# A decode step bound by its K and V loads: q from the even and odd columns of wq beside w3, the first K in two halves, rows 16 apart with one output transfer, and wo in six pieces

## The chip, the cores and the metric

The kernel runs on one core of a Trainium2 chip. The core has five engines that run their own instruction streams and meet through semaphores: TensorE (PE), VectorE (DVE), ScalarE (ACT), GpSimd (POOL) and SyncE (SP), which here issues nearly all transfers. Sixteen DMA engines move the data between the chip's main memory (HBM) and the on-chip memory (SBUF, 128 partitions); matmuls write into PSUM (eight banks of 512 fp32 values per partition). The metric is the device time of one execution in microseconds; the time of a kernel is the median of its runs. One further execution was profiled, and all durations come from that one.

## The reference

One token of each of two sequences passes a grouped-query attention over a cache of 32,768 positions, an MLP branch gates it, and the input is added.

```python
x = A_x                                   # (2, 1, 512), bf16
xn = layernorm(x)
q = xn @ wq                               # 32 heads of 128
# 8 K/V heads, each shared by 4 query heads
p = softmax(q . k_cache * 128**-0.5)      # k_cache, v_cache: (2, 8, 32768, 128), bf16
s = (p . v_cache) @ wo                    # wo: (4096, 512)
z = layernorm(xn)
h2 = gelu(z @ w3) @ w4                    # w3: (512, 1792), w4: (1792, 512)
g = silu(xn + h2)
out = x + s * g
```

In the reference's second branch there is also a term through w1 and w2 (h shifted along the sequence, then w2, added to xn before the second layernorm). With a sequence of one position all four shifts fill in zeros, so that term is zero, and the kernel leaves w1 and w2 out. The K and V caches are 268 MB of the 280.5 MB that are read.

## The kernel before

**Units.** The work is 16 units n, one for each pair of batch (n % 2) and K/V head (n // 2). Each has 8.39 MB of K and 8.39 MB of V. Both are loaded as 128 partitions of contiguous rows. `vbuf` holds one V. `kbuf` holds three halves of a K (each `CW` columns): K of an even unit lies in halves 0 and 1, of an odd unit in halves 1 and 2, and `halves(b)` gives the order in which a unit's halves are used, so that the half which the next K overwrites is used first.

**One unit.** `scores(n)`: VectorE transposes K in eight tiles of 128 x 2048 words (line 471) into two buffers `ktb`; TensorE multiplies each with the query heads in `qz` (line 483). `softmax(n)`: VectorE takes the maximum (line 496), small matmuls bring it together and spread it, ScalarE takes the exponential (line 506), VectorE transposes the weights into `pT` (line 512). `values(n)`: TensorE multiplies them with V (line 524). `unit_sum` and `unit_out` collect the unit's four heads into `oQ`; they are run inside the next unit.

**Order.** A recording layer, `Plan`, takes each operation with the regions that it reads and writes (`P.op`, line 40), works out the semaphore waits, and keeps one list for each engine in the order of recording. SyncE, ScalarE and GpSimd get their lists flat (`emit_flat`, line 97). TensorE and VectorE get loops over the units (`emit_looped`): `fit` (line 101) finds for each wait a line in the loop's counter, and waits that hold only for the first round are put ahead of the loop. TensorE's program up to the wo rows stands in a loop of two visits whose body runs in the second alone (lines 163 to 165); behind it follow the instructions from the one labelled "stop" on, the first of the wo rows.

**Transfers.** SyncE's queue holds in order: wq (into half 2 of `kbuf`), w3 (into the first columns of `vbuf`), K of unit 0 (all of it, line 337), the second half of V of unit 0, its first half (after w3 has been used), then K and V of each next unit, each waiting until its place has been used: K(n+1) for VectorE's transposes of the first-used half of K(n), V(n+1) for TensorE's `values(n)`. K of the last unit comes in two halves with the semaphores "ka" and "kb". At the end follow w4 (into half 0) and wo (into half 1), the latter in the five pieces of `wo_cuts` (line 240): 22, 4, 2, 2 and 2 rows of 512 columns on each partition.

**Head.** ScalarE issues the loads of x: `x_bf` (two rows) and `x4` (each sequence cut in four pieces of 128, put on partitions 32 j + b). Two layernorms run on VectorE with ScalarE's square root; xn and the second layernorm's result go through `xx` into `z4`, by two transfers on ScalarE's queue, in the same placing. From `z4` come `zT` (columns for the matmuls) and `xrep`. `q_job` (line 424): TensorE multiplies with wq into eight banks of 512 columns (line 432), ScalarE copies each bank to bf16 with the innermost pairs pulled apart (line 442) into `q_row`, which lies in `ktb[0]`, VectorE transposes four pieces (line 447) into `q_turn`, in `ktb[1]`, and copies out `qp` (line 449); then it clears six PSUM regions (line 453). `mlp_in` (line 555) multiplies with w3.

**Tail.** After `values(15)`: w4's product (line 608), `gather` (line 616: it adds the four partition groups by a matmul with `sel`), the last unit's sum, a transpose, and the permutation that makes `oP`, the attention result as columns by wo row (lines 649 to 656). `wo_rows` (line 626) multiplies the first rows into four partition groups of `wP`, VectorE copies these to `wsum` (line 662), and a `gather` adds the groups into `s_ps`. `wo_last` (line 637) multiplies the last rows into `s_ps` directly, in four 128-column pieces a row; the order on TensorE is rows of pieces 1 and 2, `wo_last` of pieces 3 and 4, `gather`, `wo_last` of piece 5. VectorE multiplies with the gate (line 668) and adds x (line 669), and SyncE and ScalarE each issue the output of one sequence and wait for it.

Of the kernel before, what the change touches and what calls it, by code (L numbers as in the profile page):

```python
# [26 lines left out]
class Plan:  # L27
# [3 lines left out]
    def __init__(self, nc, sems):  # L31
# [6 lines left out]
        self.turn, self.inner = {}, None  # L38
# [58 lines left out]
    def emit_flat(self, eng):  # L97
        for o in self.ops[eng]:
            self.emit_one(o, sorted(o.waits.items()))

    def fit(self, points, first):
# [17 lines left out]
        for k, w in points.items():  # L119
            for s, v in w.items():  # L120
                if k[0] == first and s not in line:
                    ahead[s] = max(ahead.get(s, 0), v)
# [46 lines left out]
    def emit_rounds(self, eng, kind, ops, first, last, ahead, rounds, segments, plans, stop):  # L169
# [6 lines left out]
        with self.nc.Fori(0, len(rounds), 1, engines=[kind], hint_back_edge=True) as i:  # L176
            for seg, fits in zip(segments, plans):
                if len(seg[0]) == 1:
                    o, line = rounds[0][seg[0][0]], fits[0]
                    self.emit_one(o, [(s, i * step + base) for s, (base, step, _) in line.items()])  # L180
# [12 lines left out]
def kernel(  # L193
# [40 lines left out]
    assert NCH == 2 and NB == NS and NU % 2 == 0 and FK <= 16 and W3 <= CW and FK * D <= CW  # L234
# [30 lines left out]
    sel = sb("sel", [128, 4, rep], F32)  # L265
    mask = sb("mask", [128, 4], F32)
    x_bf = sb("x_bf", [B, D], BF16)
    xf = sb("xf", [B, D], F32)
    xn = sb("xn", [B, D], F32)
    xx = sb("xx", [B, 4, 2, D // 4], F32)  # L270
# [3 lines left out]
    oP = sb("oP", [128, B, NR], BF16)  # L274
# [27 lines left out]
                 "wo0", "wo1", "wo2", "wo3", "wo4", "out0", "out1"]  # L302
# [14 lines left out]
    def load(sem, out_ap, in_ap, wr, rd=(), eng="SP"):  # L317
        e = {"SP": nc.sync, "ACT": nc.scalar}[eng]
        P.op(eng, lambda: e.dma_start(out=out_ap, in_=in_ap), [al(r) for r in rd],
# [14 lines left out]
    def load_k(n):  # L334
        c0 = place(n % 2, 0)
# [33 lines left out]
    for b in range(B):  # L369
        load("x4", x4[b:128:32, :], A_x[b, 0, :].rearrange("(j c) -> j c", j=4), [f"x4_{b}"],  # L370
             rd=["x4"], eng="ACT")

    dve(lambda: V.tensor_copy(out=xf[:, :], in_=x_bf[:, :]), ["x_bf"], ["xf"])
# [16 lines left out]
    layernorm(quarters(xn[:, :]), "xn", xf[:, :], "xf", 1)  # L390
    act(lambda: A.copy(out=xx[:, :, 0, :], in_=quarters(xn[:, :])), ["xn"], ["xx0"])
    dve(lambda: V.tensor_copy(out=identf[:, :], in_=ident[:, :]), ["ident"], ["identf"])
    layernorm(xx[:, :, 1, :], "xx1", xn[:, :], "xn", 2)
    for b in range(B):
        load("z4", z4[b:128:32, :, :].rearrange("j s c -> j (s c)"),
             xx[b:b + 1, :, :, :].rearrange("o j s c -> o j (s c)"), [f"z4_{b}"], rd=["xx0", "xx1", "z4"], eng="ACT")
# [8 lines left out]
    sel2 = sel[:, :, :].rearrange("p i h -> p (i h)")  # L405
    dve(lambda: V.tensor_add(out=sel2, in0=identf[:, 0:16], in1=identf[:, 32:48]), ["identf"], ["sel"])
# [308 lines left out]
```

## Time and profile before

| | |
|---|---|
| Median of 3 runs | 659.19 us (658.31 to 659.75) |
| The profiled execution | 658.29 us |
| Its span, first to last instruction | 656.3 us |
| Read from HBM | 280.50 MB, 427 GB/s over the span |
| DMA queue of SyncE (q1), share of 16 engines | 99.0% |
| TensorE matmuls busy | 401.8 us (61%) |
| VectorE busy | 385.6 us (59%) |
| ScalarE busy | 47.2 us (7%) |
| GpSimd busy | 6.7 us (1%) |
| Mean granted TensorE clock | 0.818 of full speed |

A row of the timeline gives the start and the length in microseconds, the engine, the line, the operation, the tiles (out <- in) with their shape, the count of instructions merged, and in brackets how long the engine had been idle before and what released it. PEld is the loading of weights into TensorE. "SPq" and "ACTq" are the instruction queues of SyncE and ScalarE, which issue transfers; a merged row "x2" of these runs from the first issue's start to the last one's end. A releaser is inferred: where an instruction waits for several semaphores, the last one by the profile is named.

### The profile page before, as it was taken

To read this page: it belongs to the slowest core of one execution; us is meant where nothing else is said; L and a number is where in the kernel's file an instruction comes from. 1 tells how busy PE (TensorE), PEld (TensorE's weight loads), DVE (VectorE), ACT (ScalarE), POOL (GpSimd) and SP (SyncE) were. 2 spreads that over 40 slices of the span, in tenths; PEclk is the share of its full clock that TensorE was granted. 3 is DMA by queue.
4 is the path that set the end of the run, shared out by engine and by line. 5 is a ranking of instruction groups with operands and counts; after the bars stand their busy time and mean duration, and the time that the engine had idled before them with its cause. 6 is when DMAs were issued, how large, how long until landed. Compare 5 with 4: busy or idle time off the path is not lost.

```text
span 656.3 us, 5842 instructions
## 1 busy us (share of the span) xinstructions
PE 401.8 (61%) x2291; PEld 153.4 (23%) x2291; DVE 385.6 (59%) x305; ACT 47.2 (7%) x67; POOL 6.7 (1%) x27
## 2 busy tenths in 40 slices
PE   0547583775648466573855657385565847656855
PEld 0213231231213122121322213122121312212322
DVE  4277481945739184572927648193663819367962
ACT  1910000000000000000000000000000000000011
POOL 1000000000000000000000000000000000000000
PEclk9879698776979878697886869788696978869887
DMA  8999999999999999999989999999999999999996
GB/s 365 452 417 473 387 447 431 399 447 447 447 415 415 447 447 447 403 427 447 447 387 443 448 447 439 391 447 447 447 439 391 447 447 447 431 399 445 449 402 285
DMA packets 6102, 280.54 MB, mean 427 GB/s; under 512 B 714, under 2 KB 724, under 8 KB 1236
## 3 DMA queue, kind: packets, MB, share of 16 engines
q1 hardware_dynamic: 6056, 280.50, 99.0%
q8 instruction: 1, 0.02, 0.0%
q10 hardware_dynamic: 44, 0.01, 0.0%
q14 instruction: 1, 0.01, 0.0%
HBM read 280.50 MB, written 0.00 MB: 427 GB/s over the span
## 4 chain that ended last, share of the span: by engine, by line
DMA 63%; DVE 14%; PE 14%; issue 4%; ACT 4%; ACTq 0%; POOL 0%; DVEq 0%; POOLq 0%; SPq 0%
DMA kbuf<-in_A_k_cache_dram 59%; DVE ktb L471 12%; PE banks L483 11%; DMA vbuf<-in_A_v_cache_dram 4%; ACT ktb L442 3%; PE banks L524 2%; DMA z<-xx 1%; PE banks L626 0%; PE banks L432 0%; DVE banks L453 0%; DVE acs L534 0%; ACT L658 0%; ACT L384 0%; DVE ktb L447 0%; DVE pT L512 0%
## 5 line engine op out<-in xcount | busy, mean ns | idle before, releaser
L471 DVE STREAM_TRANSPOSE ktb<-kbuf 128x2048 uint32<-128x2048 uint32 x128 | 287.3, 2288 | 164.1 <-DMA kbuf<-in_A_k_cache_dram 159.0
L483 PE MATMUL banks<-ktb,qz 128*128 128x512 bf16 x1024 | 273.1, 416 | 151.0 <-DVE ktb L471 150.3
L483 PEld LDWEIGHTS banks<-ktb,qz 128*128 128x128 bf16 x1024 | 97.2, 103 | 328.3 <-issue 186.1
L524 PE MATMUL banks<-vbuf,pT 128*16 128x512 bf16 x1024 | 89.6, 527 | 15.3 <-DVE rS L513 12.7
L524 PEld LDWEIGHTS banks<-vbuf,pT 128*16 128x16 bf16 x1024 | 31.2, 116 | 67.0 <-issue 55.9
L548 ACT CAST oQ<-banks 128x4 bf16<-128x4 f32 x16 | 2.6, 162 | 511.1 <-PE banks L545 511.1
L496 DVE TENSOR_REDUCE m<-banks 128x1 f32<-128x1024 f32 x16 | 19.6, 1225 | 32.1 <-PE banks L483 32.1
L512 DVE STREAM_TRANSPOSE pT<-pr 128x1024 bf16<-128x1024 bf16 x16 | 19.9, 1245 | 20.4 <-ACT pr L506 20.4
L509 PE MATMUL banks<-S,headf 128*128 128x1 f32 x32 | 8.0, 319 | 23.8 <-ACT pr L506 23.8
L506 ACT ACTIVATE pr<-banks,nb 128x1024 bf16<-128x1024 f32 x16 | 17.8, 1114 | 38.7 <-DVE nb L505 38.7
L432 PE MATMUL banks<-kbuf,xrep 128*128 x32 | 10.0, 486 | 15.7 <-DVE xrep L420 15.7
L442 ACT CAST ktb<-banks 128x512 bf16<-128x512 f32 x8 | 18.4, 2752 | 10.9 <-PE banks L432 10.9
L538 DVE TENSOR_REDUCE acr<-acs 128x128 f32<-128x512 f32 x17 | 17.6, 1038 | 0.6
L497 PE MATMUL banks<-identf,m 128*1 128x128 f32 x16 | 4.3, 270 | 19.2 <-DVE m L496 19.2
L534 DVE SCALAR_TENSOR_TENSOR acs<-banks,rS,mask 128x512 f32<-128x512 f32 x17 | 12.1, 714 | 4.9 <-PE banks L524 4.9
L447 DVE STREAM_TRANSPOSE ktb<-ktb 128x1024 bf16<-128x1024 bf16 x4 | 5.0, 1245 | 17.0 <-ACT ktb L442 17.0
L509 PEld LDWEIGHTS banks<-S,headf 128*128 128x128 f32 x32 | 6.6, 259 | 25.2 <-ACT pr L506 25.2
L502 PE MATMUL banks<-ones_f,gx 1*128 1x1 f32 x32 | 6.0, 256 | 9.9 <-DVE gx L500 9.9
L457 POOL TENSOR_TENSOR qz<-qp,qm 128x64 bf16<-128x64 bf16 x17 | 5.0, 293 | 623.4 <-PE banks L483 588.3
L555 PE MATMUL banks<-vbuf,zT 128*2 128x448 bf16 x16 | 3.4, 983 | 12.7 <-DVE banks L453 12.7
L432 PEld LDWEIGHTS banks<-kbuf,xrep 128*128 128x128 bf16 x32 | 3.8, 118 | 21.4 <-issue 19.3
L498 DVE TENSOR_REDUCE gm<-banks 1x4 f32<-1x128 f32 x16 | 4.5, 278 | 5.8 <-PE banks L497 5.8
(75 smaller groups left out, 60.4 us busy)
## 6 DMA issues: line engine op xcount, KB each, us to landing
vbuf<-in_A_v_cache_dram SPq DMA_DIRECT2D x2, 4096.0 KB, 30.3
kbuf<-in_A_k_cache_dram SPq DMA_DIRECT2D x2, 4096.0 KB, 22.1
kbuf<-in_A_wq_dram SPq DMA_DIRECT2D x1, 4096.0 KB, 13.4
kbuf<-in_A_wo_dram SPq DMA_DIRECT2D x1, 2816.0 KB, 31.0
vbuf<-in_B_w_dram SPq DMA_DIRECT2D x1, 1792.0 KB, 17.2
kbuf<-in_B_w_dram SPq DMA_DIRECT2D x1, 1792.0 KB, 28.1
kbuf<-in_A_wo_dram SPq DMA_DIRECT2D x3, 256.0 KB, 30.5
kbuf<-in_A_wo_dram SPq DMA_DIRECT2D x1, 512.0 KB, 30.0
```

The source lines that it names most:

```text
L432: r = T.matmul(banks[:, bass.ds(c * 512, 512)], lhsT=xrep[:, k, :, :].rearrange("p i w -> p (i w)"), rhs=kb[:, bass.ds(c * 512 + (2 * CW + ...
L442: act(lambda c=c: A.copy(out=q_row[:, 512 * c:512 * (c + 1)].rearrange("p (x two w) -> p x w two", two=2, w=32), in_=banks[:, 512 * c:512 ...
L471: dve(lambda i=i, c0=c0: V.transpose(out=ktb[i][:, :], in_=kbuf[:, c0:c0 + KG * GT * Dh].bitcast(U32)), [kreg(c0, KG * GT * Dh)], [f"ktb{i ...
L483: r = T.matmul(sc[:, bass.ds(half, HW)].rearrange("p (t k) -> p t k", k=32), lhsT=qz[:, k, off:off + 128], rhs=kv[:, k // 2, k % 2, :, :], ...
L496: dve(lambda: V.tensor_reduce(out=m1[:, :], in_=sc[:, :], axis=AX.X, op=ALU.max), ["sc"], ["m1"], "max")
L502: pe(lambda: T.matmul(bc, lhsT=gx[:, :, :].rearrange("o x h -> o (x h)"), rhs=ones_f[0:1, 0:1], start=True, stop=True), ["gx", "ones_f"], ...
L506: act(lambda: A.activation(out=pr[:, :], in_=sc[:, :], func=ACT.Exp, bias=nb[:, 0:1], scale=inv_sqrt_dh, accum_out=S1[:, :]), ["sc", "nb"] ...
L509: pe(lambda: T.matmul(sS, lhsT=headf[:, :, :].rearrange("p x h -> p (x h)"), rhs=S1[:, :], start=True, stop=True), ["headf", "S1"], [rO], "S")
L512: dve(lambda: V.transpose(out=pT[:, :, :].rearrange("p t r -> p (t r)"), in_=pr[:, :]), ["pr"], ["pT"], "pT")
L524: r = T.matmul(acc[32 * j:32 * j + 16, :].rearrange("p (i d) -> p i d", d=Dh), lhsT=pT[:, half * GT + u, r0:r0 + 16], rhs=vv[:, x, u, :, : ...
L534: dve(lambda: V.scalar_tensor_tensor(out=acs[:, :, :], in0=acc[:, :].rearrange("p (i d) -> p i d", d=Dh), scalar=rS[:, 0:1], in1=mask[:, : ...
L538: dve(lambda: V.tensor_reduce(out=acr[:, :], in_=acs[:, :, :].rearrange("p i d -> p d i"), axis=AX.X, op=ALU.add), ["acs"], ["acr"], "acr")
```

## The change

Seven edits, made together:

- **q by parities.** TensorE's product with wq takes every second column of wq as the moving operand (`[:, 0:1023:2]`), four blocks of even columns into four banks, then four of odd ones into the other four, by two nested loops. ScalarE's copies then read and write runs of 32 neighbouring values.
- **q beside w3.** `q_row` and `q_turn` lie in `vbuf` behind w3's columns instead of in `ktb`. The first half of V of unit 0, which overwrites both, waits for TensorE's product with w3 and for VectorE's copy of `qp`. `xf`, `xn` and `xx` become parts of `ktb[1]`.
- **The first K in halves.** K of unit 0 is loaded by two transfers of 4.19 MB, the half used first under "k", the other under "kb". VectorE's loop waits for "kb" at its fixed value in each round (`fixed` in `fit`).
- **Rows 16 apart.** The two sequences lie on partitions 32 j and 32 j + 16 instead of 32 j and 32 j + 1. Small products write M = 17 rows instead of 2, `oP` has 32 columns for each row of wo (cleared once on GpSimd), `sel` has 32 columns, and three of the six clears of PSUM go. `x4` is loaded by one transfer.
- **One output transfer.** SyncE issues both sequences' output as one transfer of eight rows; GpSimd waits for it, and the block is left without GpSimd's drain.
- **wo in six pieces** of 16, 8, 2, 2, 2 and 2 rows. `wo_rows` takes the first 24 rows, `wo_last` the last 8; the `gather` stands after `wo_last` of pieces 3 and 4 and ahead of pieces 5 and 6.
- **Order of writing out.** The first loads and clears of SyncE, ScalarE and GpSimd are written out ahead of TensorE's and VectorE's programs, the rest of their lists after them; each of the three engines gets a branch in between. The loop of two visits on TensorE stays.

```diff
-    wo_cuts = [0, NR - 10, NR - 6, NR - 4, NR - 2, NR]
+    wo_cuts = [0, NR - 16, NR - 8, NR - 6, NR - 4, NR - 2, NR]
...
+                if k[0] == first and s in self.fixed:
+                    line[s] = (v, 0, 0)
+                elif k[0] == first and s not in line:
                     ahead[s] = max(ahead.get(s, 0), v)
...
-        if n < NU - 1:
+        if 0 < n < NU - 1:
...
-        for sem, c in zip(("ka", "kb"), halves(n % 2)):
+        for sem, c in zip(("ka" if n else "k", "kb"), halves(n % 2)):
...
+    pool(lambda: G.memset(oP[:, :, :], 0.0), wr=["oP"])
+    load("x4", x4[0:128:16, :], A_x[:, 0, :].rearrange("b (j c) -> j b c", j=4), ["x4_0"], rd=["x4"], eng="ACT")
...
-        q_row, q_turn = (ktb[i][:, :].bitcast(BF16) for i in range(2))
+        q_row, q_turn = (vbuf[:, W3 + HD * i:W3 + HD * (i + 1)] for i in range(2))
...
-            with nc.Fori(0, 8, 1, engines=[mybir.EngineType.PE]) as c:
+            with nc.Fori(0, 2, 1, engines=pes) as e, nc.Fori(0, 4, 1, engines=pes) as h:
...
-                        rhs=kb[:, bass.ds(c * 512 + (2 * CW + k * HD), 512)],
+                        rhs=kb[:, bass.ds(h * 1024 + (e + (2 * CW + k * HD)), 1023)][:, 0:1023:2],
...
-                out=q_row[:, 512 * c:512 * (c + 1)].rearrange("p (x two w) -> p x w two", two=2, w=32),
-                in_=banks[:, 512 * c:512 * (c + 1)].rearrange("p (x w two) -> p x w two", two=2, w=32)),
+                out=q_row.rearrange("p (h x two w) -> p h two x w", h=4, two=2, w=32)[:, c % 4, c // 4, :, :],
+                in_=banks[:, 512 * c:512 * (c + 1)].rearrange("p (x w) -> p x w", w=32)),
...
-        for t, name in ((hP, "hP"), (acc, "acc"), (mD, "mD"), (wP, "wP"), (s_ps, "s_ps"), (gP, "mA")):
+        for t, name in ((acc, "acc"), (mD, "mD"), (wP, "wP")):
...
-                wP[32 * j:32 * j + B, :], lhsT=oP[:, :, r], rhs=kbuf[:, CW + r * D:CW + (r + 1) * D],
+                wP[32 * j:32 * j + M, :], lhsT=oP[:, r, 0:M], rhs=kbuf[:, CW + r * D:CW + (r + 1) * D],
...
-    for b, eng in enumerate(("SP", "ACT")):
-        load(f"out{b}", out[b, 0, :].rearrange("(j c) -> j c", j=4), out_bf[b:128:32, :], [f"out{b}"],
-             rd=["out_bf"], eng=eng)
+    load("out0", out[:, 0, :].rearrange("b (j c) -> j b c", j=4), out_bf[0:128:16, :], ["out0"], rd=["out_bf"])
...
-    with tc.tile_critical():
-        P.emit_flat("SP")
-        P.emit_flat("ACT")
-        P.emit_flat("POOL")
-        nc.sync.wait_ge(P.sems["out0"], 16)
-        nc.scalar.wait_ge(P.sems["out1"], 16)
+    with tc.tile_critical(no_gpsimd_drain=True):
+        for e, n in early.items():
+            P.emit_flat(e, 0, n)
         P.step = dict(steps, k=16, v=16)
         P.emit_looped("PE", mybir.EngineType.PE)
         P.step = {s: 2 * v for s, v in dict(steps, k=16, v=16).items()}
         P.emit_looped("DVE", mybir.EngineType.DVE)
+        for e, n in early.items():
+            P.emit_flat(e, n, None)
+        nc.gpsimd.wait_ge(P.sems["out0"], 16)
```

More of the change, by code (lines that the diff above doesn't have):

```diff
@@ L264 @@
     headm = sb("headm", [128, rep], F32)
-    sel = sb("sel", [128, 4, rep], F32)
+    sel = sb("sel", [128, 32], F32)
     mask = sb("mask", [128, 4], F32)
     x_bf = sb("x_bf", [B, D], BF16)
-    xf = sb("xf", [B, D], F32)
-    xn = sb("xn", [B, D], F32)
-    xx = sb("xx", [B, 4, 2, D // 4], F32)
+    rows = ktb[1][0:B, :].bitcast(F32)
+    xf, xn = rows[:, 0:D], rows[:, D:2 * D]
+    xx = rows[:, 2 * D:4 * D].rearrange("b (j s c) -> b j s c", j=4, s=2)
+    r_xf, r_xn, r_x0, r_x1 = (("ktb1", 2 * D * i, 2 * D * (i + 1)) for i in range(4))
     oQ = sb("oQ", [128, B, NR], BF16)
@@ L368 @@
     pool(lambda: G.memset(qz[:, :, :], 0.0), wr=["qz"])
[L369 to L373, printed above, removed]
+    pool(lambda: G.memset(oP[:, :, :], 0.0), wr=["oP"])
+    load("x4", x4[0:128:16, :], A_x[:, 0, :].rearrange("b (j c) -> j b c", j=4), ["x4_0"], rd=["x4"], eng="ACT")
+    early = {e: len(P.ops[e]) for e in ("SP", "ACT", "POOL")}
+    dve(lambda: V.tensor_copy(out=xf[:, :], in_=x_bf[:, :]), ["x_bf"], [r_xf])
     def quarters(a):
```

71 lines of the change are left out of this document (39 added, 32 removed).

## The prediction

> **What bounds the kernel now.** I read the page first (engine shares, the 40 slices, the chain that ended last), then the stages, then the DMA issues with their landings, and last the timeline of the head and of the tail.
>
> ```profile
> span 656.3 us, 5842 instructions
> DMA  8999999999999999999989999999999999999996
> q1 hardware_dynamic: 6056, 280.50, 99.0%
> DMA 63%; DVE 14%; PE 14%; issue 4%; ACT 4%; ACTq 0%; POOL 0%; DVEq 0%; POOLq 0%; SPq 0%
> L471 DVE STREAM_TRANSPOSE ktb<-kbuf 128x2048 uint32<-128x2048 uint32 x128 | 287.3, 2288 | 164.1 <-DMA kbuf<-in_A_k_cache_dram 159.0
> ```
>
> The queue of SyncE, q1, fills 99% of the span, and VectorE, which must transpose every K tile, spends 159.0 us waiting for K to land. So the first question on any edit is whether it changes the stream of bytes, and the second whether it changes what comes after the last byte. The stages (columns: stretch, length, busy time of five engines, TensorE clock, DMA share, GB/s):
>
> ```profile
> 36.00:76.00 40.00, 27.34 (x151) 9.56 (x151) 26.50 (x24) 2.66 (x5) 0.59 (x2) 0.80 1.03 439
> 76.00:116.00 40.00, 23.25 (x135) 8.91 (x135) 23.34 (x17) 1.37 (x3) 0.29 (x1) 0.84 0.98 423
> 116.00:316.00 200.00, 125.53 (x687) 47.94 (x688) 120.22 (x85) 6.84 (x15) 1.47 (x5) 0.80 1.01 435
> 636.00:650.00 14.00, 9.25 (x113) 3.44 (x115) 5.47 (x13) 2.92 (x5) 0.00 (x0) 0.74 0.94 397
> 651.00:652.00 1.00, 0.76 (x22) 0.25 (x20) 0.69 (x1) 0.00 (x0) 0.00 (x0) 0.50 0.16 59
> ```
>
> The long middle runs at 435 GB/s, and the head, 36 to 76 us, already at 439. The only weak place before the tail is 76 to 116 us with 423: at 435 its bytes would need 1.1 us less (40 x 12/435). The last bytes come just after 651 us (59 GB/s in the last row). What is left is a fixed tail of some 5 us.
>
> The SyncE issues of the head, and the landings of the four transfers after the first three (the last column of a landing row is us from issue to landing):
>
> ```profile
> 2.33 39.79 SPq L319 DMA_DIRECT2D vbuf<-in_A_v_cache_dram  x2
> 50.72 0.33 SPq L319 DMA_DIRECT2D kbuf<-in_A_k_cache_dram  x1
> 74.20 0.33 SPq L319 DMA_DIRECT2D vbuf<-in_A_v_cache_dram  x1
> ```
> ```profile
> vbuf<-in_A_v_cache_dram SPq DMA_DIRECT2D x1, 4096.0 KB, 45.2
> vbuf<-in_A_v_cache_dram SPq DMA_DIRECT2D x1, 4096.0 KB, 15.4
> kbuf<-in_A_k_cache_dram SPq DMA_DIRECT2D x1, 25.9
> vbuf<-in_A_v_cache_dram SPq DMA_DIRECT2D x1, 21.8
> ```
>
> The first row is two issues, at 2.33 and at its end, 42.12. Landings: first V half 2.33 + 45.2 = 47.5; second 42.12 + 15.4 = 57.5; K of unit 1 50.72 + 25.9 = 76.6; V of unit 1 74.20 + 21.8 = 96.0. So each transfer is issued before the one ahead of it has landed: 5.4, 6.8 and 2.4 us before. The steps between landings are 10.0, 19.1 and 19.4 us for 4.19, 8.39 and 8.39 MB, which is 419, 439 and 432 GB/s: the stream has no hole of more than 0.3 us in the head.
>
> **The change part by part.**
>
> *q by parities, beside w3.* The rows of the q stage before:
>
> ```profile
> 15.71 9.97 PE L432 MATMUL banks<-kbuf,xrep 128*128 x32 [15.71 <-DVE xrep L420]
> 17.61 18.40 ACT L442 CAST ktb<-banks 128x512 bf16<-128x512 f32 x8 [10.95 <-PE banks L432]
> 36.04 1.25 DVE L447 STREAM_TRANSPOSE ktb<-ktb 128x1024 bf16<-128x1024 bf16 x1 [3.30 <-ACT ktb L442]
> 38.34 3.40 PE L555 MATMUL banks<-vbuf,zT 128*2 128x448 bf16 x16 [12.66 <-DVE banks L453]
> 644.76 0.59 ACT L644 COPY th<-banks 128x512 f32<-128x512 f32 x1 [7.14 <-PE banks L608]
> ```
>
> ScalarE takes 18.40 us for eight copies of 512, 2.3 us each, since its innermost pair is written 64 bytes apart. With whole runs of 32 they are nearest to line 644's plain copy, 0.59 us; then TensorE's 9.97 us set the pace, the q chain ends near 15.7 + 10 + 0.6 + 1.25 + the gathering copy, about 28 us instead of 37.7, and w3's product can run from there. Three of the six clears after it go too. So the second V half (which now also waits for VectorE's gathering copy, as q lies in its target) is issued near 30 instead of 42.1, K of unit 1 near 40 instead of 50.7 and V of unit 1 near 64 instead of 74.2. All three were early enough. Bounds for the sum: 0, by the landings, and -1.1, by the 423 GB/s stretch, where the shortest lead (2.4 us) lies just ahead. I take 0, since the landings are the completions themselves, while packets of one stretch shift over its edge. If the copies stayed at 2.3 us, nothing would be lost either.
>
> *First K in halves.* One more issue of about 0.43 us on SyncE at 2 us, with 30 us of bytes queued in front of the data. VectorE could start at half a K; it is busy with q until about 28 us anyway. The constant wait on "kb" stands in every round of VectorE's loop, where the 159.0 us of waiting cover it. Cost 0; uncovered it would be eight register waits.
>
> *Rows 16 apart, M = 17.*
>
> ```profile
> L524 PEld LDWEIGHTS banks<-vbuf,pT 128*16 128x16 bf16 x1024 | 31.2, 116 | 67.0 <-issue 55.9
> 2.06 0.62 POOL L368 MEMSET qz<- 128x624 bf16 x1
> ```
>
> Weight loads of 17 columns instead of 2 run beside matmuls; the values loop's 16 columns cost 31.2/1024 = 30 ns of busy time a load, four of 2 columns in the tail (below) 0.17 us, 43 ns each: 0. The clear of oP (1,024 elements a row; qz's 624 take 0.62 us, so about 1 us) and the wider sel stand in idle stretches of GpSimd and VectorE ahead of the z transfer; a late z would shift the q chain, which has 14 us to spare. The moved head of SyncE, ScalarE and GpSimd ends in one branch each, which stands ahead of a long wait (SyncE's ended at 42.12) and costs nothing.
>
> *wo in 16, 8, 2, 2, 2, 2.* The tail, with the issues of wo's five pieces and the landing of the first (last column, from issue to landing again):
>
> ```profile
> 617.63 3.95 SPq L319 DMA_DIRECT2D kbuf<-in_A_wo_dram  x5
> kbuf<-in_A_wo_dram SPq DMA_DIRECT2D x1, 2816.0 KB, 31.0
> ```
> ```profile
> 647.37 0.23 DVE L656 CAST oP<-banks 128x64 bf16<-128x64 f32 x1 [0.30 <-PE banks L653]
> 648.73 2.28 PE L626 MATMUL banks<-kbuf,oP 128*2 128x512 bf16 x26 [1.40 <-DVE g L659]
> 648.73 0.39 PE L626 MATMUL banks<-kbuf,oP 128*2 128x512 bf16 x4 [1.40 <-DVE g L659]
> 648.94 0.60 PE L626 MATMUL banks<-kbuf,oP 128*2 128x512 bf16 x8
> 649.91 0.17 PEld L626 LDWEIGHTS banks<-kbuf,oP 128*2 128x2 bf16 x4 [0.23 <-DMA kbuf<-in_A_wo_dram]
> 651.05 0.69 DVE L662 COPY wsum<-banks 128x512 f32<-128x512 f32 x1 [2.31 <-PE banks L626]
> 651.17 0.38 PE L637 MATMUL banks<-kbuf,oP 128*2 128x128 bf16 x8
> 651.79 0.61 PE L616 MATMUL banks<-wsum,sel 128*2 128x128 f32 x8 [0.24 <-DVE wsum L662]
> 652.17 0.44 PE L637 MATMUL banks<-kbuf,oP 128*2 128x128 bf16 x8
> 652.66 0.29 DVE L668 TENSOR_TENSOR sg<-banks,g 128x128 f32<-128x128 f32 x1 [0.92 <-PE banks L637]
> ```
>
> oP is ready at 647.60, yet TensorE starts the wo rows at 648.73: the first piece, 22 rows, lands at 617.63 + 31.0 = 648.63 (the profile names g, which the product does not read). Four rows go together, 0.21 us apart. The second piece lets TensorE go on at 649.91, the fourth at 651.17: 0.63 us a piece, so the last lands near 651.75, while the sum of the earlier rows reaches TensorE only at 651.79, after 0.69 us of copying. Two bounds meet here: bytes at 651.75, and the chain rows, wsum, gather at 652.17, where the last rows start.
>
> A row is 0.131 MB, 0.30 us at 435 GB/s. The new first piece lands 6 rows earlier, 648.63 - 1.8 = 646.8, so oP sets the start: 647.65 + 3 x 0.21 + 0.39 = 648.7 for 16 rows. The next 8 land 2 rows ahead of 649.91, at 649.3, and are through at 649.9. wsum ends at 650.65. The pieces of 24 and 26 (landing 649.9 and 650.55) end at 650.95, the gather hands over at 651.35, the piece of 28 (landed 651.17) ends at 651.73, the last (landing 651.75) at 651.75 + 0.38 = 652.15. Before, sg was released at 652.63: **-0.5 us**. The bytes are the bound then, so no order of rows could give more here.
>
> The Trainium skill, "DMA: Bandwidth & Descriptors", Anatomy of one DMA, fits a DMA (issued by GpSimd, where it was measured) as about 2.0 us plus its bytes, which speaks against a sixth piece: by that, taken as serial, the sum would be 2.0 us longer. The trace does not agree with the serial reading: queued 256 KB pieces land 0.63 us apart, and their bytes alone need 0.60; it gets no chance of its own.
>
> *One output DMA, GpSimd waits.* Rows:
>
> ```profile
> 653.30 0.64 SPq L319 DMA_DIRECT2D out_dram<-out_bf  x1
> SPq L319 <- DMA out_dram<-out_bf: 1.0, 1, 1.0
> 1.86 1.16 ACTq L319 DMA_DIRECT2D x<-in_A_x_dram  x2
> ```
> ```profile
> 652.63 0.02 issue
> ```
>
> The issue ends at 653.94, the output has landed at 654.94, and 1.36 us follow to the span's end. Before, SyncE waited, then told the others, heard from all and went on; now all have reported before, and only GpSimd's word to SyncE is left. That saves one exchange of several in 1.36 us: bounds 0 and -0.5; I take -0.15, as a released engine goes on at once here (the last row, of the chain: 0.02 us from TensorE's end to sg). Eight rows in one DMA instead of four in each of two queues: the x issues are 0.58 for 4 rows, and 128 rows of K are issued in 0.33, so more rows do not lengthen an issue: 0. If four more rows cost as much again as the first four, it would be +0.64 + 1.0 = +1.6.
>
> **Sum**: 0 (head) - 0.5 (wo) - 0.15 (end) = -0.65 us on the profiled execution, 658.29 (span 656.3 and 2.0 around it), so 657.65. That execution was 0.9 below the median of the runs, 659.19; against the median it is 658.5. A difference under 0.2% (1.3 us) is about what a measurement of this kernel can't tell from none.
>
> **The rivals.**
>
> 1. *The head did cost something.* If the short lead of 2.4 us ahead of V of unit 1 left some of the sixteen DMA engines dry, the weak stretch, 1.1 us, comes back, and everything to the end moves with it: 658.5 - 1.1 = 657.4. For it speaks 423 beside 439 and 435; against it, the 19.1 and 19.4 us steps of the landings.
>
> 2. *The wo rows do not start earlier.* TensorE leaves its two-visit loop between the perm product (before 647.37) and the wo rows, and until 648.63 that was hidden. If the code behind the branch is what is late next, the start stays at 648.73: 16 rows to 649.75, 8 more to 650.4, wsum 651.15, gather at 651.2 to 651.6, two pieces to 652.4: -0.2, with the end 658.85. The Trainium skill, "Runtime: NRT & Kernel Launch", Instruction fetch mechanics, says that a taken branch to code outside the window makes the sequencer fetch it first. No row here shows what that costs at this place.
>
> 3. *Slower: the output in one queue.* If rows behind one another in one queue cost what they cost side by side, the +1.6 above falls on the last link, where nothing hides it: 659.19 - 0.5 + 1.6 = 660.3. It decides from +0.65 upwards. Against it speaks that issue times here do not grow with rows.
>
> **How the numbers follow.** The forecast has 0.50, its own range 657.9 to 659.2; rival 1 0.20, rival 2 0.18, rival 3 0.12. Faster by over 0.2% means under 657.87: most of rival 1 (0.16) and the low edge of the forecast (0.06), 0.22. Slower means over 660.5: about two thirds of rival 3, since its own price is a bound from rows that are not the same, and a little of the rest, 0.10. Within: 0.68. The range runs from 657.1, below rival 1, to 660.2, short of most of rival 3.
>
> **What would show it.** In the profile after: the q copies near 0.6 us each, the first K transposes near 29 us, V of unit 1 issued near 64 us, and yet the last V landing within half a microsecond of 637.7; the stretch 76 to 116 us at 435 would be rival 1. In the tail wo rows from 647.65 (from 648.7: rival 2), sg at about 652.2, and from the output's issue to the end of the span 2.85 us instead of 3.0 (over 3.7: rival 3). I am wrong if the last V lands elsewhere by more than a microsecond: the stream then depends on something I took as fixed.

## The result, and the profile after

| | before | changed |
|---|---|---|
| Median, 7 runs each, taken side by side | 659.19 us (657.92 to 659.96) | 657.0 us (656.69 to 657.71) |
| Profiled execution | 658.29 us | 656.69 us |
| Its span | 656.3 us | 654.9 us |

The ratio is 0.997, with a 95% interval from 0.9958 to 0.9982; by the medians the change is faster by 2.2 us, 0.33%. The forecast was 658.5, its own range 657.9 to 659.2, the stated range 657.1 to 660.2. The median lies 0.1 us under the low end of that range, and nearest to rival 1 (657.4), which had 0.20. It is on the side "faster by over 0.2%", which had 0.22; the weak end of the interval, 0.18%, just misses that mark.

The page of the changed kernel, the lines that answer to those of before:

```profile
span 654.9 us, 5862 instructions
DMA  8999999999999999999999999999999999999996
q1 hardware_dynamic: 6348, 280.50, 99.1%
DMA 73%; DVE 14%; PE 7%; issue 5%; SPq 0%; DVEq 0%
L488 DVE STREAM_TRANSPOSE ktb<-kbuf 128x2048 uint32<-128x2048 uint32 x128 | 286.8, 2286 | 172.9 <-DMA kbuf<-in_A_k_cache_dram 170.7
```

The same bytes in the same queue, which is as full as before. VectorE's waiting for K grew from 159.0 to 170.7 us: what the head does earlier ends in more waiting for data. The stages (stretch, length, busy time of the five engines, clock, DMA share, GB/s):

```profile
36.00:76.00 40.00, 20.09 (x126) 7.88 (x124) 17.69 (x14) 2.65 (x4) 0.29 (x1) 0.79 1.03 444
76.00:116.00 40.00, 23.21 (x135) 8.89 (x135) 23.52 (x17) 1.37 (x3) 0.29 (x1) 0.84 1.00 433
116.00:316.00 200.00, 125.30 (x689) 47.98 (x690) 120.48 (x85) 6.84 (x15) 1.47 (x5) 0.81 1.00 433
```

The weak stretch, 76 to 116 us, went from 423 to 433 GB/s, the rate of the middle. That was the sign given for rival 1. A row counts each packet whole, in the stretch in which it starts, so a long row can gain or lose packets at its edges. Rows of 2.42 us don't have this fault in a full stream, as that is the time of one packet of 65,536 bytes on each of the sixteen DMA engines at 433 GB/s. Around the seam between K and V of unit 1 they read, in before (first fence) and in the changed kernel (second):

```profile
73.62:76.04 2.42, 0.53 (x12) 0.03 (x4) 0.00 (x0) 0.00 (x0) 0.00 (x0) 1.00 1.25 433
76.04:78.46 2.42, 0.00 (x0) 0.00 (x0) 1.78 (x1) 0.00 (x0) 0.00 (x0) 0.54 0.56 244
```
```profile
76.04:78.46 2.42, 0.00 (x0) 0.00 (x0) 1.85 (x1) 0.00 (x0) 0.00 (x0) 0.50 1.00 433
```

In before, the packets that start in the first row take 1.25 times as long as in a full stream (the DMA share, the last column but one), and in the second row seven of the sixteen engines start none: 2.42 x (1 - 244/433) = 1.06 us are missing, as a mean over the engines. The changed kernel has no such hole.

The head, in the timeline of the changed kernel (start, length, engine, line, count, idle before and its releaser) and the issues of SyncE with the landing of V of unit 1 and of the last V (last column: us from issue to landing):

```profile
18.18 0.59 ACT L458 CAST vbuf<-banks 128x512 bf16<-128x512 f32 x1 [10.90 <-PE banks L448]
31.06 4.47 DVE L488 STREAM_TRANSPOSE ktb<-kbuf 128x2048 uint32<-128x2048 uint32 x2
2.90 28.17 SPq L326 DMA_DIRECT2D vbuf<-in_A_v_cache_dram  x2
41.69 0.33 SPq L326 DMA_DIRECT2D kbuf<-in_A_k_cache_dram  x1
63.88 0.33 SPq L326 DMA_DIRECT2D vbuf<-in_A_v_cache_dram  x1
610.85 0.33 SPq L326 DMA_DIRECT2D vbuf<-in_A_v_cache_dram  x1
```
```profile
vbuf<-in_A_v_cache_dram SPq DMA_DIRECT2D x1, 32.0
vbuf<-in_A_v_cache_dram SPq DMA_DIRECT2D x1, 26.0
```

Copies of 0.59 us, K of unit 1 issued at 41.69 (before: 50.72) and V of unit 1 at 63.88 (before: 74.20). V of unit 1 landed at 63.88 + 32.0 = 95.9, 0.1 us earlier than before, and the last V at 610.85 + 26.0 = 636.85, 0.8 us earlier than the 637.65 of before. In this pair of executions the landing of V of unit 1, the last of its sixteen completions, shows 0.1 of these 0.8 us; the rest is lost later in the one execution of before (0.4 us of it in one step between landings, which took 19.7 us where its neighbours take 19.3), far from any edit, and is not explained. So this pair alone doesn't tell what the head is worth.

The tail of the changed kernel, in its timeline:

```profile
646.91 0.43 DVE L673 CAST oP<-banks 128x64 bf16<-128x64 f32 x1 [0.30 <-PE banks L670]
647.40 1.70 PE L643 MATMUL banks<-kbuf,oP 128*17 128x512 bf16 x24 [0.53 <-DVE oP L673]
649.15 0.69 DVE L681 COPY wsum<-banks 128x512 f32<-128x512 f32 x1 [0.87 <-PE banks L643]
649.90 0.41 PE L633 MATMUL banks<-wsum,sel 128*17 128x128 f32 x8
651.07 0.29 PE L654 MATMUL banks<-kbuf,oP 128*17 128x128 bf16 x8 [0.34 <-DMA kbuf<-in_A_wo_dram]
651.41 0.29 DVE L688 TENSOR_TENSOR sg<-banks,g 128x128 f32<-128x128 f32 x1 [1.57 <-PE banks L654]
652.06 0.69 SPq L326 DMA_DIRECT2D out_dram<-out_bf  x1
```

The wo rows start 0.06 us behind the end of oP's copy (647.34) and no longer wait for bytes; the copy to `wsum` and the gather are done before the last piece, and the last thing waited for is a piece of wo. The chain that ended last says the same, in its last part (start, length, what):

```profile
619.89 31.13 DMA kbuf<-in_A_wo_dram
651.02 0.04 issue
651.07 0.32 PE banks L654 x8
```

From the last V's landing to `sg` it is 651.41 - 636.85 = 14.56 us, where it was 652.66 - 637.65 = 15.01. From the output's issue to the end of the span it is 654.9 - 652.06 = 2.84 us (3.00 before), and 1.8 us lie outside the span (2.0 before).

### The profile page after: what moved, and what is told of

It reads as the page before. It is cut to its first block, busy times and chain, and to the rows that moved or that the text cites. A ratio compares the mean times of both kernels' runs of the same rounds, so it can differ in the third digit from the quotient of the medians.

```text
span 654.9 us, 5862 instructions
## 1 busy us (share of the span) xinstructions
PE 397.9 (61%) x2297; PEld 152.0 (23%) x2297; DVE 384.6 (59%) x302; ACT 33.5 (5%) x67; POOL 7.6 (1%) x28
## 3 DMA queue, kind: packets, MB, share of 16 engines
q1 hardware_dynamic: 6348, 280.50, 99.1%
## 4 chain that ended last, share of the span: by engine, by line
DMA 73%; DVE 14%; PE 7%; issue 5%; SPq 0%; DVEq 0%
DMA kbuf<-in_A_k_cache_dram 69%; DVE ktb L488 13%; PE banks L500 7%; DMA kbuf<-in_A_wo_dram 5%; DVE acs L551 1%; SPq L326 0%; DVE acr L555 0%; DVEq L90 0%; PE banks L654 0%; DVE sg L688 0%; DVE out_bf L689 0%; SPq L728 0%; SPq L693 0%
## 5 line engine op out<-in xcount | busy, mean ns | idle before, releaser
L488 DVE STREAM_TRANSPOSE ktb<-kbuf 128x2048 uint32<-128x2048 uint32 x128 | 286.8, 2286 | 172.9 <-DMA kbuf<-in_A_k_cache_dram 170.7
L500 PE MATMUL banks<-ktb,qz 128*128 128x512 bf16 x1024 | 268.2, 410 | 164.8 <-DVE ktb L488 164.1
L500 PEld LDWEIGHTS banks<-ktb,qz 128*128 128x128 bf16 x1024 | 95.6, 102 | 338.6 <-issue 189.6
L529 DVE STREAM_TRANSPOSE pT<-pr 128x1024 bf16<-128x1024 bf16 x16 | 19.9, 1245 | 20.4 <-ACT pr L523 20.4
L463 DVE STREAM_TRANSPOSE vbuf<-vbuf 128x1024 bf16<-128x1024 bf16 x4 | 4.9, 1234 | 8.6 <-ACT vbuf L458 8.5
L519 PEld LDWEIGHTS banks<-ones_f,gx 1*128 1x128 f32 x32 | 5.0, 196 | 13.0 <-DVE gx L517 13.0
L522 DVE TENSOR_SCALAR nb<-banks 128x1 f32<-128x1 f32 x16 | 2.5, 158 | 7.8 <-PE banks L519 7.8
```

The costliest lines, as they stand in the source:

```text
L488: dve(lambda i=i, c0=c0: V.transpose(out=ktb[i][:, :], in_=kbuf[:, c0:c0 + KG * GT * Dh].bitcast(U32)), [kreg(c0, KG * GT * Dh)], [f"ktb{i ...
L500: r = T.matmul(sc[:, bass.ds(half, HW)].rearrange("p (t k) -> p t k", k=32), lhsT=qz[:, k, off:off + 128], rhs=kv[:, k // 2, k % 2, :, :], ...
L519: pe(lambda: T.matmul(bc, lhsT=gx[:, :, :].rearrange("o x h -> o (x h)"), rhs=ones_f[0:1, 0:1], start=True, stop=True), ["gx", "ones_f"], ...
L529: dve(lambda: V.transpose(out=pT[:, :, :].rearrange("p t r -> p (t r)"), in_=pr[:, :]), ["pr"], ["pT"], "pT")
```

## The experiments

The theories at the start were three: the head gained after all (V of unit 1 was issued too late in the runs of before), or the wo pieces gained more than the 0.5 us given to them, or the end did. Times are medians with their range and number of runs; each kernel ran side by side with the kernel before. That kernel had 658.82 (657.13 to 661.28, 35 runs) beside the first four, 658.71 (657.57 to 660.44, 22) beside the middle four, and 658.71 (657.13 to 660.22, 25) beside the last four, which ran on another chip than the first eight.

**The wo pieces alone.** Edit of before:

```diff
-    wo_cuts = [0, NR - 10, NR - 6, NR - 4, NR - 2, NR]
+    wo_cuts = [0, NR - 16, NR - 8, NR - 6, NR - 4, NR - 2, NR]
...
+    wo_last(wo_cuts[5], wo_cuts[6])
```

> The kernel before with wo in 16, 8, 2, 2, 2, 2 rows and the gather ahead of the last two pieces, nothing else. By the sum of the prediction: 0.5 us faster than before, wo rows from about 647.7 counted on the profile before (right behind oP), last rows released by the landing of the last piece. If the gain of the whole change (2.2 us between the medians) comes from the wo pieces, 1.5 us or more. If the code behind the two-visit loop were late, 0.2 us and a start 1.1 us behind oP.

Measured: 657.84 us (656.99 to 658.46, 12 runs), ratio 0.9984 [0.9973, 0.9995]: 1.0 us, about twice the term, with an interval from 0.3 to 1.8 us, in which the term itself lies. Its timeline and three of its stretches:

```profile
646.71 1.04 PE L626 MATMUL banks<-kbuf,oP 128*2 128x512 bf16 x16 [0.32 <-DVE oP L656]
652.06 0.29 DVE L669 TENSOR_TENSOR sg<-banks,g 128x128 f32<-128x128 f32 x1 [1.20 <-PE banks L637]
```
```profile
76.00:116.00 40.00, 24.69 (x135) 9.51 (x135) 23.04 (x17) 1.37 (x3) 0.29 (x1) 0.82 0.97 421
73.62:76.04 2.42, 0.00 (x0) 0.00 (x0) 0.00 (x0) 0.00 (x0) 0.00 (x0) 1.00 1.22 433
76.04:78.46 2.42, 0.00 (x0) 0.00 (x0) 1.72 (x1) 0.00 (x0) 0.00 (x0) 0.90 0.90 379
```

The wo rows start right behind oP, without the other edits. The weak stretch stays weak (421), so it belongs to the old head; by the short rows the hole is smaller here, 0.3 us (379 of 433 GB/s).

**The head alone.** Before with q by parities in `vbuf` and with the first K in halves:

```diff
-        q_row, q_turn = (ktb[i][:, :].bitcast(BF16) for i in range(2))
+        q_row, q_turn = (vbuf[:, W3 + HD * i:W3 + HD * (i + 1)] for i in range(2))
...
-                        rhs=kb[:, bass.ds(c * 512 + (2 * CW + k * HD), 512)],
+                        rhs=kb[:, bass.ds(h * 1024 + (e + (2 * CW + k * HD)), 1023)][:, 0:1023:2],
...
-        for sem, c in zip(("ka", "kb"), halves(n % 2)):
+        for sem, c in zip(("ka" if n else "k", "kb"), halves(n % 2)):
```

> The kernel before with q by parities beside w3 and the first K in halves, nothing else. By the sum: the same time as before (0, at most 0.2 us faster, as the landings of the second V differ by 0.1 us in the two profiles). By rival 1 (the 2.4 us lead ahead of V of unit 1 left engines dry): 0.8 to 1.1 us faster, and the runs lie closer together than those of before.

Measured: 657.88 us (656.96 to 658.54, 12 runs), ratio 0.9983 [0.9973, 0.9993]: 0.9 us, where the sum had 0. The stage:

```profile
76.00:116.00 40.00, 24.53 (x135) 9.41 (x135) 23.50 (x17) 1.37 (x3) 0.29 (x1) 0.80 1.01 436
```

So the head did cost something, and it alone lifts the weak stretch from 423 (before) to 436.

**The end alone.** GpSimd waits for both outputs (two transfers, as before), and the block has no drain of GpSimd:

```diff
-    with tc.tile_critical():
+    with tc.tile_critical(no_gpsimd_drain=True):
...
-        nc.sync.wait_ge(P.sems["out0"], 16)
-        nc.scalar.wait_ge(P.sems["out1"], 16)
+        nc.gpsimd.wait_ge(P.sems["out0"], 16)
+        nc.gpsimd.wait_ge(P.sems["out1"], 16)
```

> The kernel before with GpSimd waiting for both outputs and no GpSimd drain, nothing else: both output transfers stay. By the sum: 0.15 us faster, and 2.85 us instead of 3.0 from the output's issue to the end of the span. If the end carries the unexplained part, 0.5 us or more.

Measured: 658.88 us (657.71 to 660.24, 12 runs), ratio 0.9999 [0.9989, 1.0008]. Its output is issued at 653.36, 2.94 us before its span ends (656.3), against 3.00. A gain of up to 0.7 us is within the interval, so this bears out no more than that the end is small.

**The changed kernel, without its head.** Changed, with the old q stage in `ktb` and the first K in one transfer (`q_row`, the product with wq, ScalarE's copies and the semaphores as in the lines with a minus above; the other edits stay).

> The changed kernel with the old q stage (contiguous columns of wq, q in ktb, pairs pulled apart by ScalarE) and the first K in one transfer; everything else as changed. By the sum: the time of the changed kernel, 657.0 (0 to 0.2 us above). By rival 1: 0.8 to 1.1 us above, about 658.

Measured: 657.14 us (656.8 to 659.42, 12 runs), ratio 0.9982 [0.9971, 0.9993], beside the changed kernel at 656.88 (in the next group, on the same chip). By the median the head is then worth 0.26 us, by the means (657.50 and 656.90) 0.6. Eight runs lie up to 657.52, four between 657.6 and 659.4. In its profile the second half of V of unit 0 is issued at 32.8 us (before: 41.8), V of unit 1 at 72.98, and that lands at 96.08, on time. By its median this run bears out the sum and not rival 1: most of its runs lose nothing, though V of unit 1 is issued no earlier than in the profiles of the wo pieces alone and the end alone (72.6). It is not the old head in full, as the second half of V of unit 0 goes out 9 us earlier; whether that is why, no run here shows.

**The changed kernel again.**

> The changed kernel once more, as it is, beside the kernels that follow on the same chip. 657.0, as before, and 1.8 to 2.2 us under the kernel before.

Measured: 656.88 us (656.65 to 657.12, 7 runs), ratio 0.9972 [0.9960, 0.9983]. The spread is the news: a standard deviation of 0.16 us, where before has 0.67.

**The changed kernel with the old wo pieces.**

```diff
-    wo_cuts = [0, NR - 16, NR - 8, NR - 6, NR - 4, NR - 2, NR]
+    wo_cuts = [0, NR - 10, NR - 6, NR - 4, NR - 2, NR]
...
-    wo_last(wo_cuts[5], wo_cuts[6])
```

> The changed kernel with wo in its old five pieces (22, 4, 2, 2, 2), everything else as changed. By the sum and by the run with the pieces alone (0.98 us between the medians): 0.5 to 1.0 us above the changed kernel, the wo rows starting about 1.1 us behind oP. If the pieces are worth nothing beside the other parts: the same time.

Measured: 657.70 us (656.77 to 658.64, 11 runs), ratio 0.9986 [0.9976, 0.9995], 0.8 us above the changed kernel, again more than 0.5. Yet its profiled execution has `sg` as early as the changed kernel's:

```profile
648.06 1.68 PE L643 MATMUL banks<-kbuf,oP 128*17 128x512 bf16 x26 [1.12 <-DMA kbuf<-in_A_wo_dram]
651.44 0.29 DVE L687 TENSOR_TENSOR sg<-banks,g 128x128 f32<-128x128 f32 x1 [0.97 <-PE banks L654]
```

The clock tells why. One stretch of the tail, from the first wo rows to `sg`, in this kernel (first fence) and in before (second); the last three columns are the granted clock, the DMA share and GB/s:

```profile
648.00:651.50 3.50, 2.77 (x58) 1.12 (x58) 1.05 (x3) 0.02 (x1) 0.00 (x0) 1.00 0.50 193
```
```profile
648.60:652.60 4.00, 3.63 (x58) 1.44 (x58) 0.83 (x2) 0.00 (x0) 0.00 (x0) 0.63 0.65 253
```

With the old pieces the 26 rows take 1.68 us at full clock, and 3.15 where the clock is low, as in the profile of the head alone, whose pieces are the old ones too (the stretch, then the rows):

```profile
648.00:652.60 4.60, 3.93 (x58) 1.69 (x58) 0.71 (x2) 0.00 (x0) 0.00 (x0) 0.65 0.35 133
```
```profile
648.09 3.15 PE L633 MATMUL banks<-kbuf,oP 128*2 128x512 bf16 x26 [2.04 <-DMA kbuf<-in_A_wo_dram]
651.28 0.69 DVE L669 COPY wsum<-banks 128x512 f32<-128x512 f32 x1 [3.82 <-PE banks L633]
652.59 0.29 DVE L675 TENSOR_TENSOR sg<-banks,g 128x128 f32<-128x128 f32 x1 [0.61 <-PE banks L644]
```

The changed kernel, too, had a low clock in about the same stretch, in the profile of its second measurement (stretch and rows):

```profile
647.60:651.90 4.30, 2.79 (x48) 1.10 (x48) 0.95 (x2) 0.00 (x0) 0.00 (x0) 0.50 0.46 178
```
```profile
648.61 1.03 PE L643 MATMUL banks<-kbuf,oP 128*17 128x512 bf16 x8 [1.15 <-DMA kbuf<-in_A_wo_dram]
649.70 0.69 DVE L681 COPY wsum<-banks 128x512 f32<-128x512 f32 x1 [2.39 <-PE banks L643]
651.64 0.29 DVE L688 TENSOR_TENSOR sg<-banks,g 128x128 f32<-128x128 f32 x1 [1.25 <-PE banks L654]
```

It is hardly held up by it: at half the clock `wsum` is copied by 650.39, ahead of the last piece, and `sg` starts at 651.64, behind that. From the last V's landing to `sg`: old pieces 14.5 us (this kernel, full clock), 15.0 (before), 15.6 (the head alone and the end alone, low clock). New pieces 14.5 to 14.7 in every profile, whatever the clock.

**V of unit 1 made late.** Now the head's mechanism itself. The changed kernel with N more copies on ScalarE ahead of those of q; they write a scratch tile that is rewritten before it is read, so nothing is left out. They delay q, and with it all of unit 0 and the issues of the second half of V of unit 0, of K of unit 1 and of V of unit 1; the rest of the code is unchanged.

```diff
+        for _ in range(31):
+            act(lambda: A.copy(out=th[:, :], in_=kbuf[:, 2 * CW:2 * CW + 512]), [kreg(2 * CW, 512)], ["th"])
```

With N = 31:

> The changed kernel with 31 copies of 0.6 us put on ScalarE ahead of the q copies (into a tile that is rewritten later), so that V of unit 1 is issued near 74.3 us as in the profile before, instead of 63.9. If the lead of that transfer matters (rival 1): 0.5 to 1.1 us above the changed kernel, and the first of the sixteen DMA engines reaches the end of that V about 1 us later than 19.3 us after the end of the K ahead of it. If it doesn't: the same time within 0.2 us.

Measured: 659.92 us (658.83 to 660.61, 11 runs), ratio 1.0020 [1.0011, 1.0029]: 3.0 us above the changed kernel. V of unit 1, issue and landing (last column):

```profile
77.14 0.33 SPq L326 DMA_DIRECT2D vbuf<-in_A_v_cache_dram  x1
```
```profile
vbuf<-in_A_v_cache_dram SPq DMA_DIRECT2D x1, 22.0
```

With N = 35:

> The same with 35 copies: V of unit 1 issued near 76.7 us, when the K ahead of it has just landed. By rival 1: every DMA engine is dry for some time, 2 to 3 us above the changed kernel. By the sum of the prediction, too, a hole of 2 us or more, as the stream has no cover left there; it tells what one microsecond of lateness costs.

Measured: 661.92 us (661.25 to 663.28, 5 runs), ratio 1.0051 [1.0036, 1.0065].

```profile
79.64 0.33 SPq L326 DMA_DIRECT2D vbuf<-in_A_v_cache_dram  x1
```
```profile
vbuf<-in_A_v_cache_dram SPq DMA_DIRECT2D x1, 22.1
```

Both issues came about 3 us later than the number of copies was meant to give, so that both lie beyond the point in question. They settle what lies there: with nothing in front of it, V takes 22.0 us from issue to landing (77.14 + 22.0 = 99.1; 79.64 + 22.1 = 101.7), and the time follows about one for one (N = 31 lands 3.1 us after the changed kernel's 96.07 and ends 3.0 us later; N = 35 is issued another 2.5 us later, lands 2.6 and ends 2.0 us later). Not all of it arises at V: K of unit 1, issued late as well, lands at 77.0 and 78.7 instead of 76.7. In the full stream V of unit 1 lands at 96.0, so it has to be issued by 96.0 - 22.0 = 74.0. The profile of before has it at 74.20, on the wrong side.

With N = 24 and with N = 26, to come near that point from the good side:

> The changed kernel with 24 copies ahead of the q copies: V of unit 1 issued near 72.8 us, 3.9 us ahead of the landing of K of unit 1 (76.7), where the kernel before stood in two of the profiles. The two late issues of the runs before (77.1 and 79.6 us) cost 3.1 and 5.7 us at that V's landing, one microsecond for each: on that line the cost begins at 74.0. If it begins sharply there: the changed kernel's time, 656.9. If the runs of the kernel before lose their 0.9 us here, run by run: 657.3 to 657.8, with a wider spread than the changed kernel's 0.16.

> The same with 26 copies: V of unit 1 issued near 74.0 us. Sharp beginning: 656.9 to 657.1. With the spread of the issue over the runs: 657.6 to 658.2, the runs wider apart.

Measured: 657.13 us (656.87 to 658.01, 9 runs), ratio 0.9975 [0.9965, 0.9985], and 657.81 us (656.75 to 658.96, 11 runs), ratio 0.9993 [0.9983, 1.0003]. The first lies between its two forecasts, the second is as forecast for an issue that spreads over the runs. In the profiles V of unit 1 was issued at 71.68 and at 72.53, about 1.3 us earlier than meant, and landed on time, at 96.2 and 96.0; so what the median of N = 26 loses (0.9 us) is not seen in its profile. By the issue in the profile the medians make one row (N = 24 and 26 ran on the other chip, where the kernel of the last experiment, the changed one but for one row of wo, has 656.92):

| V of unit 1 issued (profile) | median | standard deviation of the runs |
|---|---|---|
| 64.6 (changed) | 656.88 | 0.16 |
| 71.7 (N = 24) | 657.13 | 0.35 |
| 72.5 (N = 26) | 657.81 | 0.68 |
| 77.1 (N = 31) | 659.92 | 0.52 |
| 79.6 (N = 35) | 661.92 | 0.81 |

Flat while there is cover, one for one without it, and between these a zone in which some runs lose and others don't, so that the spread grows fourfold; it stays wide beyond. That fits an issue time that differs from run to run. The profiles show that it does: with the same head, the profiles of the wo pieces alone and of the end alone have this issue at 72.63 and 72.62, that of before at 74.20. Most of the 1.6 us arises in the scores of unit 0, where TensorE was at 0.58 of its clock in before and at full clock in the other (the same stretch and its matmuls, in before and with the wo pieces alone):

```profile
48.40:51.40 3.00, 2.84 (x8) 1.07 (x9) 2.29 (x2) 0.00 (x0) 0.00 (x0) 0.58 0.88 382
48.56 5.32 PE L483 MATMUL banks<-ktb,qz 128*128 128x512 bf16 x16 [2.03 <-DVE ktb L471]
```
```profile
48.40:51.40 3.00, 2.72 (x12) 1.07 (x13) 3.00 (x2) 0.00 (x0) 0.00 (x0) 1.00 0.96 415
48.39 1.91 PE L483 MATMUL banks<-ktb,qz 128*128 128x512 bf16 x8 [2.03 <-DVE ktb L471]
50.58 1.91 PE L483 MATMUL banks<-ktb,qz 128*128 128x512 bf16 x8 [0.28 <-DVE ktb L471]
```

The sixteen matmuls end at 53.88 in before and at 52.49 in the other, 1.4 us apart.

**Before with head and pieces, without the rest.**

> The kernel before with the two parts that gained alone, head (q by parities beside w3, first K in halves) and the six wo pieces, without the rest (rows 16 apart, one output, GpSimd's wait, order of writing out). If the two add up and the rest is worth nothing: 1.7 to 1.8 us under the kernel before, the changed kernel's time within 0.2 us. If the rest carries something: 0.3 us or more above the changed kernel.

Measured: 657.23 us (656.76 to 657.42, 9 runs), ratio 0.9976 [0.9966, 0.9985]. V of unit 1 is issued at 63.73 and lands at 95.83; the output is issued 3.2 us before the end of the span. So these two parts carry 1.5 of the 1.8 us, and 0.3 is left for the rest together: the rows 16 apart, the one output, GpSimd's wait and the order of writing out. Its rows show 0.4 us of that between the output's issue and the end (3.2 against 2.85).

**A last piece of one row.** Changed with `NR - 1` for the last `NR - 2`, pieces of 16, 8, 2, 2, 3 and 1 rows.

> The changed kernel with wo in 16, 8, 2, 2, 3, 1 rows. Behind the last landing stand four 128-column products instead of eight: where the landing is the bound, 0.1 us under the changed kernel; where the chain over wsum is the bound (TensorE at half clock), the same time.

Measured: 656.92 us (656.62 to 657.2, 7 runs), ratio 0.9970 [0.9959, 0.9982], the changed kernel's time. No kernel here beat it.

## Where the prediction was right and where it failed, by its own steps

That the change is small was forecast rightly; its size was not, 0.7 us against 2.2. That the stated range comes within 0.1 us of the median is owed to rival 1, for whose sake it reached down to 657.1; the forecast's own mechanism gave 658.5. One of the three terms failed outright.

- **Head: 0, the step that failed.** It measured 0.9 us alone. The issue times forecast were right (V of unit 1 near 64); the failure is the sentence "All three were early enough", and the test behind it: that a transfer is early enough if it is issued before the one ahead has landed. V of unit 1 was, by 2.4 us. But V needs 22.0 us from its issue when nothing holds it up, and 19.4 us after the landing of the one ahead in a full stream, so it must lead by at least 2.6 us. The row with 21.8 us from issue to landing, the shortest of the head's transfers of 8.39 MB, was on show: that is the time of a transfer that had nothing left in front of it. The landings were no evidence against a loss either, since they are the last of sixteen completions, and since the one execution looked at stood just at the edge; it stood 0.9 below the median of the runs, and runs in which the clock fell otherwise would lose more. This last step is inferred: the issue times of the runs without a profile are not known.
- **Rival 1** named the place, the mechanism (a lead of 2.4 us that leaves some of the sixteen DMA engines dry) and the price, 1.1 us, and the late issues bear it out. In the trace of before the first of the sixteen completions of V of unit 1 came 20.4 us after the first of those of K, the last 19.4 us after the last; in the changed kernel both steps are 19.3. So the engines that were ahead did run dry, by about 1.1 us, as the row with 244 GB/s shows too, and the landing, which is the last completion, hid it: that execution lost 0.1 us there and had no cover left. The prediction set the 423 GB/s aside as packets shifted over the stretch's edge. Such shifts exist (N = 24, whose V landed on time, shows 426 in the same stretch), but here the missing packets were real, and rows one packet long tell the two apart.
- **A misread row.** The prediction put the second issue of the merged row at its end, 42.12; the row ends with the last issue's end, so the issue was at 41.79. That half of V then landed at 57.2, and the steps between landings are 9.7, 19.4 and 19.4 us instead of 10.0, 19.1 and 19.4. The 0.3 us that seemed to be missing there were not, and nothing else hangs on it.
- **wo: -0.5, right in kind, too small.** It measured -1.0 alone (interval 0.3 to 1.8, so the run alone doesn't exclude 0.5) and +0.8 when taken out of the changed kernel. The start behind oP, the gather ahead of the last pieces and the bytes as the bound all came as described. What was mis-sized is the kernel before: its order was costed with the clock of one execution, 15.0 us from the last V to `sg`, while it takes 14.5 to 15.6, as the clock falls over its 26 rows (2.28 us for them at a granted clock of 0.70 in before, 1.68 at 1.00 and 3.15 at 0.51 in the two profiles above). The new order takes 14.5 to 14.7, so the term is 0 to -1.0 by the execution, and the pair of profiles shows one draw from it.
- **End: -0.15, right in its row.** Output issue to end 2.84 us (forecast 2.85), and 2.8 to 2.9 in the other kernels with one output, 3.0 to 3.2 with two (2.96 in the end alone). The median of the end alone shows no gain (658.88 beside 658.82) and is too wide to exclude one. The 0.2 us less outside the span don't come from the end: the wo pieces alone and the head alone, with the old end, have 1.8 us there too.
- **The costs set to nothing** held where a row shows them: 17 columns, the clear of oP and the second issue for the first K appear nowhere on the chain. oP's own copy grew from 0.23 to 0.43 us (it writes 32-column steps), which the list had left out.
- **Rival 2** fell: TensorE goes on 0.06 us behind oP, with the exit of its loop just ahead. The Trainium skill's fetch for a taken branch ("Runtime: NRT & Kernel Launch", Instruction fetch mechanics) is not visible there; if it is paid, then while TensorE waits.
- **Rival 3** fell: eight rows are issued in 0.69 us where four took 0.64.
- **A sixth piece**, against which the Trainium skill's fixed 2.0 us for a DMA was weighed ("DMA: Bandwidth & Descriptors", Anatomy of one DMA), cost nothing that shows: TensorE takes up the four last pieces at 649.11, 649.75, 650.43 and 651.07, 0.6 to 0.7 us apart, so that behind one another in a queue they don't pay it each. A stream that has run empty pays 2.6 us once, as above.
- **What "within 0.2%" rested on:** two terms, by the medians 0.5 and 0.9 too small in the same direction. By means, the parts alone give -0.87 (head), -0.87 (wo) and +0.07 (end), together -1.7 beside the changed kernel's -1.8. Head and pieces in one kernel gave -1.4, within the intervals of these parts.

What stays open: the wo pieces alone and the end alone lost 0.45 and 0.3 us at V of unit 1 in their profiles (landing at 96.5 and 96.2) though it was issued at 72.6, while the changed kernel with N = 26 lost nothing with 72.5. So a lead of 2.6 us is not always enough: these two had 4.1 and 3.9. Their engines didn't wait long, but the packets that started between 73.62 and 76.04 us took 1.22 and 1.16 times as long as in a full stream (1.02 with N = 26). They differ in when the second half of V of unit 0 is issued (41.6 against 38.7, and 32.8 in the changed kernel without its head, which lost nothing there either), and in more. That the runs without a profile lose their time at V of unit 1 is inferred from the runs with N more copies, not seen. How the head's gain divides between q, the halves of K and that issue was not separated.

## What to carry to other kernels

Before a prefetch is called early enough, take the shortest time from issue to landing of transfers of that size and compare the lead with what exceeds the step between landings; that is the least it must be, and here two with 1.3 and 1.5 us more still lost 0.3 and 0.45 us. A transfer that shows that shortest time has no cover left, even where its landing looks on time; rows of the stream as long as one packet show whether engines ran dry. Where a tail's order depends on TensorE's pace, cost it at both clocks that the profiles show, since one execution shows one draw. A wide spread of the runs beside a narrow one after an edit (0.67 and 0.16 us here) can itself be a sign that a bound stood at its edge.

## What the runs showed of the hardware that was not expected

- A load of 8.39 MB takes 22.0 to 22.1 us from issue to landing into a stream that has run empty (N = 31 and 35), and lands 19.3 to 19.4 us behind another one in a full stream. The difference, 2.6 us, is the least lead that keeps the stream whole; with leads of 4.1 and 3.9 us two profiles still lost 0.45 and 0.3 us.
- TensorE's granted clock over the same few microseconds differs between executions of programs that are alike there: 0.58 and 1.00 at 48.4 to 51.4 us. With it an issue moved by 1.6 us, and the tail with the old wo pieces by up to 1.1 (14.5 us from the last V to `sg` where the clock was 1.00 and the 26 rows took 1.68 us, 15.6 where they took 3.15). The Trainium skill, "TensorE: Matmul & The Clock Gate", Part 1, says that the window in which the activity is measured runs freely, so that the same kernel sees it at another phase each time. The two rows above are consistent with it; they don't show the window itself.
- The landing of a transfer, its last completion, can look on time (0.1 us late) while engines that were ahead have stood dry for 1.1 us: the row of 2.42 us showed it (244 against 433 GB/s), and the landing didn't.
